# Half-lane products in a spectral token stage, a warm-up on a constant, and another order in the head of a fused LayerNorm, FFT-filter and GeGLU kernel

## Chip, cores and metric

The kernel runs on one core of a Trainium2 chip. The metric is device time in microseconds (us), the median of several executions. A core has TensorE (PE, matrix products, with its weight loads shown as PEld), VectorE (DVE), ScalarE (ACT), GpSimd (POOL) and SyncE (SP). The engines run on their own instruction streams, in order, and wait for each other with semaphores. In this kernel SP issues nearly all transfers; ACT issues a few at the start.

## The reference, cut to what matters

`A_x` is 2048 rows (tokens) of 512. It is normalised per row; the result `xn` goes two ways: through a 2-D real FFT, a product with a complex filter and the inverse FFT (A), and through a gated layer with 1792 hidden columns (B). The sum of `x`, A and B is stored.

```python
def _A_ref(x, w_r, w_i):
    X = rfft2(x.astype(f32), axes=(-2, -1))
    X = X * (w_r + 1j * w_i)
    return irfft2(X, s=(S, D), axes=(-2, -1)).astype(bf16)

def _B_ref(x, w_gate, w_up, w_down):
    g = einsum("bsd,df->bsf", x, w_gate)
    u = einsum("bsd,df->bsf", x, w_up)
    return einsum("bsf,fd->bsd", gelu_tanh(g) * u, w_down)

xn = layernorm(x)            # per row, eps 1e-5, no scale or shift
return x + _A_ref(xn, A_w_r, A_w_i) + _B_ref(xn, B_w_gate, B_w_up, B_w_down)
```

## The kernel before

**Planner.** The kernel function doesn't write the instruction streams directly. It lists operations with `op(engine, cost, fn, reads, writes, tiles, key, after, due)`. `_Sched.run` then plays through a model of the engines: of the operations that can start soonest on an engine (within `SLACK`), it takes the one with the least `due`, or, without one, the least readiness time plus `key`. Readiness of a PE operation of the spectral way gets `MARGIN` (1.0) on top once the model's time is past 12. A transfer (`dma`) goes through one modelled pipe of `RATE` bytes per us, and its end is the pipe's. `after` and the list `gate` add dependences: every SP load made after an entry in `gate` waits for that entry. The order found is emitted; at run time the engines follow it and wait on semaphores, whatever the model thought of times.

**Data.** The 2048 rows are 16 blocks of 128 rows (`x[:, s]`, partition = row within the block). Each block gets statistics (`stats`: L520, L521 on DVE), an inverse root (`root_act`: L525 on ACT and the reciprocal L527 on DVE, for blocks 0 and 1; `root_pool`: L532 and L533 on POOL for the others) and is normalised into `specB` (`norm`, L537; block 0 in two halves in `first_half`, L570). The blocks 0 to 3 are turned on PE with the identity matrix (L567 and L550) and copied out of PSUM to `xnT` (L572, L555); blocks 4 to 15 are turned by transfers (`turn_dma`, L576 on SP).

**The head.** PE starts with products on a tile of zeros into a bank nobody reads (L476, "warming"): eight in `warms` and two more inside the loop over blocks 0 and 1. DVE makes that tile of zeros. ACT issues the load of the identity and the first quarter of the transform constants (`small[:, 0:2]`), then the first 384 columns of the two gated weights `wg` and `wu`. SP issues the row blocks 0 and 1, waits for the third warming product (`gate`), and issues blocks 2 and 3, columns 384 to 768 of `wg` and `wu`, rows 4 to 7, and so on. `first` (L737) makes the first three feature columns' products for blocks 0 and 1, one block at a time; then come the products of `gated` (L718), 256 or 512 rows wide, with gelu (L723; L751 in `first`) and a copy (L724; L752) on ACT and the product of both on DVE (L725; L753). `down` (L766) multiplies by `wd`. These gated and down products are the filler of PE's stream: they have keys above 1000 and are taken whenever nothing of the spectral way is due.

**The spectral way.** `mirror` and `fold` combine groups of four row blocks on DVE. `mirror(b)` subtracts two mirrored parts and turns the difference, for b > 0 with a transfer on SP (L592), into `odd[b]`; `fold(b)` uses `odd[b]` in two of its operations. The channel transform is on PE (L631). A first part of the token transform is done on DVE (the long series of L466, the line of the helper `tt`, and L809), the rest on PE in eight classes `v`: `f_t`, two 512-column products for v > 0 (L851), and four for v = 0 (L854), which holds the two special classes 0 and 8: lanes 0 to 63 and 64 to 127 of its four stationary matrices are for either, with zeros in the other half. ACT copies each class out (L859). Then the filter product on DVE, the inverse token transform on PE (L931, L932), a DVE series, and the inverse channel transform (L991). The columns 0 and 256 need sums and differences of filter values, `edge`, made on POOL (L864) and used in six small DVE operations per half (L898).

**The filter loads.** After the transposes SP loads `wd`, the token constants `tf`, the filter in 22 transfers (`W`, spans of 14 to 460 KB), nine small ones for special rows, and the inverse constants `ti`. `gate` holds them behind an operation in `mirror(3)`: `hold[16] = sch.ops[-2]`, the subtraction that feeds the transfer of `odd[3]`.

Of the kernel before, what the change touches and what calls it, by code (L numbers as in the profile page):

```python
# [15 lines left out]
P = 128  # L16
# [3 lines left out]
WARM = 8  # L20
HKEY = 1.5
NORM = 14.0, 1.5
# [117 lines left out]
class _Op:  # L140
    __slots__ = ("eng", "fn", "cost", "key", "lag", "reads", "writes", "preds", "tiles", "first", "end", "pos", "dma", "seq",
                 "extra", "due")


class _Sched:
# [11 lines left out]
    def op(self, eng, cost, fn, reads=(), writes=(), tiles=(), key=0.0, after=(), dma=0, lag=0.0, due=None):  # L157
        o = _Op()
        o.eng, o.fn, o.cost, o.key, o.dma, o.lag, o.due = eng, fn, cost, key, dma, lag, due
# [41 lines left out]
    def run(self):  # L201
# [15 lines left out]
        while todo:  # L217
# [26 lines left out]
            if o.dma:  # L244
# [104 lines left out]
def bass_parallel_sum__spectral_gfnet__glu_gated_geglu__prompt_kernel(  # L349
# [24 lines left out]
    with ExitStack() as es:  # L374
# [30 lines left out]
        zero = sb("zero", [512])  # L405
# [54 lines left out]
        def dma(q, dst, src, nbytes, wr=None, rd=None, key=0.0, after=(), cost=0.41, lag=0.0):  # L460
            after = tuple(after) + tuple(gate if q == "sp" else ())
            return op(q, cost, lambda e: e.dma_start(dst() if callable(dst) else dst.ap, src() if callable(src) else src.ap),
                      reads=rd if rd is not None else (), writes=wr if wr is not None else (), dma=nbytes, key=key, after=after, lag=lag)
# [6 lines left out]
        op("dve", 0.2, lambda e: e.memset(zero.ap, 0.0), writes=(zero,), key=-90)  # L470


        wt = _T("dn")

        def warm(key):
            return op("pe", 0.427, lambda e: e.matmul(ps_dn[:, :], zero.ap[:, 0:P], zero.ap, start=True, stop=True), reads=(zero,), tiles=(wt,), key=key)  # L476

        warms = [warm(-50) for _ in range(WARM)]


# [7 lines left out]
        def rows(lo, hi):  # L488
            return load("sp", x[:, lo:hi], xb[:, lo:hi, :], (hi - lo) * 131072, key=next(k))
# [33 lines left out]
        def root_act(s0, n, key):  # L523
# [3 lines left out]
            op("dve", 0.09, lambda e: e.reciprocal(rs.ap[:, sl], rs.ap[:, sl]), reads=(rs[:, sl],), writes=(rs[:, sl],), key=key)  # L527
# [29 lines left out]
        def first_half(h):  # L557
# [14 lines left out]
            op("dve", 0.21, lambda e: e.tensor_copy(o.ap, bank()), writes=(o,), tiles=(t,), key=-70.0)  # L572
# [11 lines left out]
        odd = {}  # L584
# [22 lines left out]
        def fold(b):  # L607
# [9 lines left out]
            tt(f[:, :, 2], f[:, :, 3], odd[b], SUB, 512, kk)  # L617
            tt(f[:, :, 3], f[:, :, 3], odd[b], ADD, 512, kk)
# [46 lines left out]
        for s in range(4, 16):  # L665
# [3 lines left out]
            if s % 4 == 3:  # L669
                mirror(s // 4)  # L670
                hold[16] = sch.ops[-2]
# [6 lines left out]
        gate.append(hold[16])  # L678
# [364 lines left out]
```

## Time and profile before

| | us |
|---|---|
| median of 3 runs | 171.83 (171.66 to 171.91) |
| the profiled execution | 172.02 |
| its span in the profile | 170.0 |
| DVE, ACT, POOL busy | 146.1, 106.0, 11.5 |
| first warming product starts | 1.17 |
| first product of `first` starts | 6.11 |
| first product of `gated` starts | 9.44 |
| products of L854 (class 0) | 65.8 to 66.8 |
| last product ends | 167.7 |

Three lines of the costliest groups and two of the transfers:

```profile
L718 PE MATMUL ps_gu<-xnT,wg 128*128 128x512 bf16 (+1 forms) x236 | 56.7, 363 | 0.0
L718 PE MATMUL ps_gu<-xnT,wu 128*128 128x512 bf16 (+1 forms) x236 | 56.7, 363 | 0.0
...
L520 DVE BATCH_NORM_STATS2 bst<-x_sb 128x6 f32<-128x512 bf16 x16 | 10.9, 684 | 2.6 <-DMA x_sb<-in_A_x_dram 2.6
...
wg<-in_B_w_gate_dram SPq DMA_DIRECT2D x2, 512.0 KB, 8.7
wu<-in_B_w_up_dram SPq DMA_DIRECT2D x2, 512.0 KB, 9.2
```

A group line reads: line, engine, operation, output <- inputs, shapes, count | total busy us, mean ns of one | idle time of the engine just before them and what ended it. Matmuls are pipelined: a 512-column product is shown with 0.379, but the next one starts 0.216 later, so what counts for PE's stream is the distance of the starts. A transfer line reads: output <- input, queue, count, size, and the median time from issue to landing.

### The profile page before, as it was taken

What the parts mean: (1) busy time and instruction counts of PE and PEld (TensorE: products, weight loads), DVE (VectorE), ACT (ScalarE), POOL (GpSimd) and SP (SyncE); (2) the same over time, 40 slices, a digit from 0 to 9 for tenths busy, and PEclk for the clock granted to TensorE, in tenths of its full rate; (3) what the DMA queues carried; (4) which work ended last, traced back from release to release, by engine and by line L of the source; (5) the groups of instructions that cost most, each with busy time, mean ns of one, the idle gap of its engine ahead of it and who ended that gap; (6) DMA issues with size and microseconds to landing.
All of it is one profiled execution on the core that took longest, in us unless ns stands there. A gap on an engine that the chain in (4) does not pass through costs nothing.

```text
span 170.0 us, 2695 instructions
## 1 busy us (share of the span) xinstructions
PE 166.2 (98%) x998; PEld 85.9 (51%) x998; DVE 146.1 (86%) x295; ACT 106.0 (62%) x173; POOL 11.5 (7%) x23
## 2 busy tenths in 40 slices
PE   7999999999999999999999999999999999999994
PEld 2588544445556444444444465554445664444453
DVE  2879999796945999999999999999999969963931
ACT  3478776573977758588854696795637896561000
POOL 2022242500000000400000000000000000000000
DMA  5999989974975435000000000000000002300321
GB/s 145 344 346 348 277 176 327 189 211 83 121 128 125 85 53 198 0 6 0 0 0 0 0 4 0 0 0 0 4 0 2 0 4 99 128 19 0 123 68 62
DMA packets 22239, 15.62 MB, mean 92 GB/s; under 512 B 9165, under 2 KB 21714, under 8 KB 22226
## 3 DMA queue, kind: packets, MB, share of 16 engines
q1 hardware_dynamic: 21026, 14.60, 38.0%
q10 hardware_dynamic: 1200, 0.85, 1.6%
q8 instruction: 8, 0.13, 0.3%
q14 instruction: 5, 0.04, 0.1%
HBM read 11.38 MB, written 2.10 MB: 79 GB/s over the span
## 4 chain that ended last, share of the span: by engine, by line
PE 95%; DMA 3%; DVE 1%; issue 0%; DVEq 0%
PE ps_gu L718 55%; PE ps_dn L766 21%; PE ps_sp L766 7%; DMA x_sb<-in_A_x_dram 3%; PE ps_sp L631 2%; PE ps_sp L991 2%; PE ps_sp L851 2%; PE ps_sp L931 1%; PE ps_sp L932 1%; PE ps_dn L476 1%; PE ps_gu L737 1%; PE ps_sp L854 1%; DVE bst L520 0%; PE ps_dn L737 0%; PE ps_sp L550 0%; DVE xnT L555 0%
## 5 line engine op out<-in xcount | busy, mean ns | idle before, releaser
L718 PE MATMUL ps_gu<-xnT,wg 128*128 128x512 bf16 (+1 forms) x236 | 56.7, 363 | 0.0
L718 PE MATMUL ps_gu<-xnT,wu 128*128 128x512 bf16 (+1 forms) x236 | 56.7, 363 | 0.0
L723 ACT ACTIVATE gg<-ps_gu 128x512 bf16<-128x512 f32 (+1 forms) x59 | 33.7, 571 | 14.3 <-PE ps_gu L718 12.1
L724 ACT ACTIVATE uu<-ps_gu 128x512 bf16<-128x512 f32 (+1 forms) x59 | 33.9, 574 | 10.5 <-PE ps_gu L718 10.2
L766 PE MATMUL ps_dn<-wd,hT 128*128 128x512 bf16 x168 | 39.0, 379 | 0.0
L466 DVE TENSOR_TENSOR specB<-specB 128x512 bf16<-128x512 bf16 (+2 forms) x58 | 33.1, 609 | 3.8 <-DMA specB<-specB 2.3
L718 PEld LDWEIGHTS ps_gu<-xnT,wu 128*128 128x128 bf16 x236 | 22.8, 98 | 23.2
L718 PEld LDWEIGHTS ps_gu<-xnT,wg 128*128 128x128 bf16 x236 | 22.6, 98 | 22.3 <-ACT uu L752 0.2
L766 PEld LDWEIGHTS ps_dn<-wd,hT 128*128 128x128 bf16 x168 | 16.2, 98 | 18.6
L725 DVE TENSOR_TENSOR hT<-gg,uu 128x512 bf16<-128x512 bf16 (+1 forms) x59 | 22.6, 393 | 1.7 <-ACT uu L724 1.6
L774 ACT ACTIVATE db<-ps_dn 128x512 bf16<-128x512 f32 x12 | 7.2, 597 | 17.7 <-PE ps_dn L766 17.7
L520 DVE BATCH_NORM_STATS2 bst<-x_sb 128x6 f32<-128x512 bf16 x16 | 10.9, 684 | 2.6 <-DMA x_sb<-in_A_x_dram 2.6
L466 DVE TENSOR_TENSOR specC<-specB 128x1024 bf16<-128x1024 bf16 (+2 forms) x18 | 12.4, 712 | 0.2
L766 PE MATMUL ps_sp<-wd,hT 128*128 128x512 bf16 (+2 forms) x70 | 12.3, 336 | 0.0
L466 DVE TENSOR_TENSOR specB<-specA 128x2048 bf16<-128x2048 bf16 x8 | 9.4, 1217 | 1.4 <-ACT specA L636 1.4
L466 DVE TENSOR_TENSOR specB<-specB,filt 128x2048 bf16<-128x2048 bf16 x8 | 9.4, 1219 | 0.0
L766 PEld LDWEIGHTS ps_sp<-wd,hT 128*128 128x128 bf16 x70 | 6.3, 98 | 6.1 <-DVE x_sb L777 0.2
L775 DVE TENSOR_TENSOR x_sb<-db,x_sb 128x512 bf16<-128x512 bf16 x12 | 5.0, 418 | 4.8 <-ACT db L774 4.7
L859 ACT ACTIVATE specA<-ps_sp 128x1024 bf16<-128x1024 f32 x8 | 8.0, 1035 | 1.5 <-PE ps_sp L851 1.3
L996 ACT ACTIVATE specB<-ps_sp 128x1024 bf16<-128x1024 f32 x8 | 7.8, 1031 | 0.4 <-PE ps_sp L991 0.4
L937 ACT ACTIVATE specC<-ps_sp 128x1024 bf16<-128x1024 f32 x8 | 7.8, 1034 | 0.3 <-PE ps_sp L932 0.3
L636 ACT ACTIVATE specA<-ps_sp 128x1024 bf16<-128x1024 f32 x8 | 7.8, 1031 | 0.0
(71 smaller groups left out, 128.9 us busy)
## 6 DMA issues: line engine op xcount, KB each, us to landing
out_dram<-x_sb SPq DMA_DIRECT2D x15, 128.0 KB, 1.8
wd<-in_B_w_down_dram SPq DMA_DIRECT2D x1, 1792.0 KB, 8.7
x_sb<-in_A_x_dram SPq DMA_DIRECT2D x3, 512.0 KB, 8.5
wg<-in_B_w_gate_dram SPq DMA_DIRECT2D x2, 512.0 KB, 8.7
wu<-in_B_w_up_dram SPq DMA_DIRECT2D x2, 512.0 KB, 9.2
toki<-c_ti SPq DMA_DIRECT2D x1, 768.0 KB, 4.7
tokf<-c_tf SPq DMA_DIRECT2D x1, 576.0 KB, 4.4
x_sb<-in_A_x_dram SPq DMA_DIRECT2D x4, 128.0 KB, 3.6
```

The lines of the kernel that those rows point to most:

```text
L466: return op("dve", c_tt(n), lambda e: e.tensor_tensor(o.ap, a.ap, b.ap, f), reads=(a, b), writes=(o,), key=key, **kw)
L520: op("dve", 0.61, lambda e: e.bn_stats(bst[:, s].ap, xs(s).ap), reads=(xs(s),), writes=(bst[:, s],), key=key, due=due, after=after)
L636: op("act", c_act(1024), lambda e, yv=yv, t=t: e.activation(yv.ap, spair(t).rearrange("p (s r i) -> p s i r", s=4, r=4), ACT.Copy), writes ...
L718: ins = e.matmul(gub(t, n), w.ap[:, dc, fc * P:(fc + 1) * P], xnT.ap[:, b, sl, dc, :], start=(dc == 0), stop=(dc == 3))
L723: op("act", c_act(n), lambda e: e.activation(gg.ap[:, gs.slot, 0:n], gub(g, n), ACT.Gelu_apprx_tanh), tiles=(g, gs), key=0.0)
L724: op("act", c_act(n), lambda e: e.activation(uu.ap[:, us.slot, 0:n], gub(u, n), ACT.Copy), tiles=(u, us), key=0.0)
L725: op("dve", c_tt(n), lambda e: e.tensor_tensor(hT.ap[:, h.slot, lo:lo + n], gg.ap[:, gs.slot, 0:n], uu.ap[:, us.slot, 0:n], MUL), tiles=(g ...
L766: ins = e.matmul(bank(), hT.ap[:, hs[(b, fc)].slot, sl * P:(sl + 1) * P], wd.ap[:, fc, lo:lo + n], start=(fc == 0), stop=(fc == NFC - 1))
L774: op("act", c_act(n), lambda e: e.activation(db.ap[:, d.slot, 0:n], bank(), ACT.Copy), tiles=(t, d), key=0.0)
L859: op("act", c_act(1024), lambda e, xv=xv, t=t: e.activation(xv.ap, spair(t), ACT.Copy), writes=(xv,), tiles=(t,), key=-0.5)
L937: op("act", c_act(1024), lambda e, gv=gv, t=t: e.activation(gv.ap, spair(t).rearrange("p (k x i) -> p k x i", k=4, x=4), ACT.Copy), writes ...
L996: op("act", c_act(1024), lambda e, rv=rv, t=t: e.activation(rv.ap, spair(t), ACT.Copy), writes=(rv,), tiles=(t,), key=-0.5)
```

## The change

Six things are changed together.

1. **Class 0.** The four products of `f_t` for v = 0 use only the 64 lanes that aren't zero: for i = 0, 1 and r = 0, 1 lanes 64r to 64r + 63 of the stationary matrix and of `H`. The order is now r inside i. The planner counts two products for it instead of four.
2. **Warming** multiplies a constant 1.0, which the framework keeps in a small tile set by POOL before the kernel starts, broadcast to 512 columns. The zero tile and its memset go. There are ten products of 512 columns and one of 256, all in `warms`; the two in the loop go. The gate of SP's third and later loads is the fourth warming product instead of the third.
3. **Loads.** The identity goes from ACT's queue to SP's, behind blocks 0 and 1. Four loads get a fixed landing time for the planner (`land`): these don't move the modelled pipe on.
4. **Order of statistics and roots.** Block 1's reciprocal root and block 0's get other keys, and block 0's reciprocal waits for block 1's statistics. Blocks 2 and 3 take their statistics after block 1 is normalised, turned and copied, and their roots on POOL are taken one by one. Statistics of blocks 4 to 15 wait for the norm of block 3. The norms' due times start at 15 instead of 14.
5. **Copies.** The two halves of block 0 are copied out of PSUM by ACT instead of DVE, and the first use of gelu (L643, which makes ACT load its table) waits for them.
6. **The filter loads' gate** is now the operation in `fold(3)` that subtracts `odd[3]`, thus behind the landing of its transfer (`turned[3]`).

```diff
-WARM = 8
+WARM = 10 * (512,) + (256,)
-NORM = 14.0, 1.5
+NORM = 15.0, 1.5
...
-            if o.dma:
+            if o.land:
+                o.end = o.land
+            elif o.dma:
                 pipe = max(pipe, st + 1.9) + o.dma / RATE
                 o.end = pipe + 0.4 + o.lag
...
-        op("dve", 0.2, lambda e: e.memset(zero.ap, 0.0), writes=(zero,), key=-90)
+        ones = nc.const_aps.tensor(1.0, (P, 512), BF16)
...
-            return op("pe", 0.427, lambda e: e.matmul(ps_dn[:, :], zero.ap[:, 0:P], zero.ap, start=True, stop=True), reads=(zero,), tiles=(wt,), key=key)
+            return op("pe", 0.000834 * n, lambda e: e.matmul(ps_dn[:, 0:n], ones[:, 0:P], ones[:, 0:n], start=True, stop=True), tiles=(wt,), key=-50)
-        warms = [warm(-50) for _ in range(WARM)]
+        warms = [warm(n) for n in WARM]
...
-        load("act", small[:, 0:2].rs([2 * P]), c_small.ap()[:, 0:2 * P], 65536, key=-9)
         for w, v in ((wg, wgv), (wu, wuv)):
-            wload("act", w, v, 0, 384, key=0.5)
+            wload("act", w, v, 0, 384, key=0.5, land=5.5 if w is wg else 6.4)
         rows(0, 1)
         rows(1, 2)
-        gate.append(warms[2])
+        load("sp", small[:, 0:2].rs([2 * P]), c_small.ap()[:, 0:2 * P], 65536, key=next(k))
+        gate.append(warms[3])
         for i in (2, 3):
-            rows(i, i + 1)
+            rows(i, i + 1, 6.3 + 0.3 * i)
...
-            op("dve", 0.09, lambda e: e.reciprocal(rs.ap[:, sl], rs.ap[:, sl]), reads=(rs[:, sl],), writes=(rs[:, sl],), key=key)
+            op("dve", 0.09, lambda e: e.reciprocal(rs.ap[:, sl], rs.ap[:, sl]), reads=(rs[:, sl],), writes=(rs[:, sl],), key=key, after=after)
...
-            op("dve", 0.21, lambda e: e.tensor_copy(o.ap, bank()), writes=(o,), tiles=(t,), key=-70.0)
+            op("act", 0.3, lambda e: e.activation(o.ap, bank(), ACT.Copy), writes=(o,), tiles=(t,), key=-70.0)
...
             tt(f[:, :, 2], f[:, :, 3], odd[b], SUB, 512, kk)
+            turned[b] = sch.ops[-1]
...
         stats(0, -60.0)
-        stats(1, -55.0, None, (sch.ops[-1],))
-        root_act(0, 1, -60.0)
-        root_act(1, 1, -58.0)
-        op("act", 1.5, lambda e: e.activation(tmp.ap, eps.ap, ACT.Gelu_apprx_tanh), reads=(eps, rs[:, 0:2]), writes=(tmp,), key=-30.0)
+        stats(1, -66.0, None, (sch.ops[-1],))
+        root_act(0, 1, -75.0, (sch.ops[-2],))
+        root_act(1, 1, -64.0)
         for h in range(2):
             first_half(h)
-        for s in range(2):
-            if s:
-                norm(s, -60.0)
-                turn(s, 1, -60.0)
-            warm(-30)
-            if s == 0:
-                stats(2, -30.0, None, (sch.ops[-2],))
-        stats(3, -30.0, None, (sch.ops[-2],))
-        root_pool(2, 2, -50.0)
+        op("act", 1.5, lambda e: e.activation(tmp.ap, eps.ap, ACT.Gelu_apprx_tanh), reads=(eps, xnT[:, 0, 0], rs[:, 0:2]), writes=(tmp,), key=-30.0)
+        norm(1, -60.0)
+        turn(1, 1, -60.0)
         for s in (2, 3):
+            stats(s, -58.0, None, (sch.ops[-1],))
+        for s in (2, 3):
+            root_pool(s, 1, -50.0)
             norm(s, -50.0)
+            early = sch.ops[-1]
             turn(s, 1, -50.0)
...
         for s in range(4, 16):
-            stats(s, 0.0, STAT[0] + STAT[1] * (s - 4))
+            stats(s, 0.0, STAT[0] + STAT[1] * (s - 4), (early,))
...
-                hold[16] = sch.ops[-2]
...
-        gate.append(hold[16])
+        gate.append(turned[3])
...
-                for r in range(2):
-                    if v:
-                        ins = e.matmul(spb(t, r), tf.ap[:, 2 + 2 * v + r], H.ap[:, hh[r]], start=True, stop=True)
-                    else:
-                        for i in range(2):
-                            ins = e.matmul(spb(t, r), tf.ap[:, 2 * r + i], H.ap[:, hh[i]], start=(i == 0), stop=(i == 1))
+                for r in range(2) if v else ():
+                    ins = e.matmul(spb(t, r), tf.ap[:, 2 + 2 * v + r], H.ap[:, hh[r]], start=True, stop=True)
+                for i in range(0 if v else 2):
+                    for r in range(2):
+                        l = slice(64 * r, 64 * r + 64)
+                        ins = e.matmul(spb(t, r), tf.ap[l, 2 * r + i], H.ap[l, hh[i]], start=(i == 0), stop=(i == 1))
                 return ins
-            op("pe", (2 if v else 4) * mm(512), f_t, reads=(H[:, hh[0]], H[:, hh[1]], tf), tiles=(t,), lag=0.1)
+            op("pe", 2 * mm(512), f_t, reads=(H[:, hh[0]], H[:, hh[1]], tf), tiles=(t,), lag=0.1)
```

More of the change, by code (lines that the diff above doesn't have):

```diff
@@ L141 @@
     __slots__ = ("eng", "fn", "cost", "key", "lag", "reads", "writes", "preds", "tiles", "first", "end", "pos", "dma", "seq",
-                 "extra", "due")
+                 "extra", "due", "land")
 class _Sched:
@@ L155, in pool, with op @@
         self.pools[name] = n
-    def op(self, eng, cost, fn, reads=(), writes=(), tiles=(), key=0.0, after=(), dma=0, lag=0.0, due=None):
+    def op(self, eng, cost, fn, reads=(), writes=(), tiles=(), key=0.0, after=(), dma=0, lag=0.0, due=None, land=None):
         o = _Op()
-        o.eng, o.fn, o.cost, o.key, o.dma, o.lag, o.due = eng, fn, cost, key, dma, lag, due
+        o.eng, o.fn, o.cost, o.key, o.dma, o.lag, o.due, o.land = eng, fn, cost, key, dma, lag, due, land
         o.reads, o.writes, o.tiles = reads, writes, [(t, False) for t in tiles]
@@ L404, in bass_parallel_sum__spectral_gfnet__glu_gated_geglu__prompt_kernel @@
         t2 = sb("edge2", [2, 4, 2])
-        zero = sb("zero", [512])
         eps = sb("eps", [1], F32)
@@ L458, in bass_parallel_sum__spectral_gfnet__glu_gated_geglu__prompt_kernel, with dma @@
         gate = []
-        def dma(q, dst, src, nbytes, wr=None, rd=None, key=0.0, after=(), cost=0.41, lag=0.0):
+        def dma(q, dst, src, nbytes, wr=None, rd=None, key=0.0, after=(), cost=0.41, lag=0.0, land=None):
             after = tuple(after) + tuple(gate if q == "sp" else ())
             return op(q, cost, lambda e: e.dma_start(dst() if callable(dst) else dst.ap, src() if callable(src) else src.ap),
-                      reads=rd if rd is not None else (), writes=wr if wr is not None else (), dma=nbytes, key=key, after=after, lag=lag)
+                      reads=rd if rd is not None else (), writes=wr if wr is not None else (), dma=nbytes, key=key, after=after, lag=lag, land=land)
         def tt(o, a, b, f, n, key=0.0, **kw):
@@ L468, in bass_parallel_sum__spectral_gfnet__glu_gated_geglu__prompt_kernel, with warm @@
         ADD, SUB, MUL = ALU.add, ALU.subtract, ALU.mult
-        op("dve", 0.2, lambda e: e.memset(zero.ap, 0.0), writes=(zero,), key=-90)
+        ones = nc.const_aps.tensor(1.0, (P, 512), BF16)
         wt = _T("dn")
-        def warm(key):
-            return op("pe", 0.427, lambda e: e.matmul(ps_dn[:, :], zero.ap[:, 0:P], zero.ap, start=True, stop=True), reads=(zero,), tiles=(wt,), key=key)
-        warms = [warm(-50) for _ in range(WARM)]
+        def warm(n):
+            return op("pe", 0.000834 * n, lambda e: e.matmul(ps_dn[:, 0:n], ones[:, 0:P], ones[:, 0:n], start=True, stop=True), tiles=(wt,), key=-50)
+        warms = [warm(n) for n in WARM]
         def load(q, dst, src, nbytes, **kw):
@@ L487, in bass_parallel_sum__spectral_gfnet__glu_gated_geglu__prompt_kernel, with rows @@
         k = iter(np.arange(0.0, 1.0, 0.001))
-        def rows(lo, hi):
-            return load("sp", x[:, lo:hi], xb[:, lo:hi, :], (hi - lo) * 131072, key=next(k))
-        load("act", small[:, 0:2].rs([2 * P]), c_small.ap()[:, 0:2 * P], 65536, key=-9)
+        def rows(lo, hi, land=None):
+            return load("sp", x[:, lo:hi], xb[:, lo:hi, :], (hi - lo) * 131072, key=next(k), land=land)
         for w, v in ((wg, wgv), (wu, wuv)):
-            wload("act", w, v, 0, 384, key=0.5)
+            wload("act", w, v, 0, 384, key=0.5, land=5.5 if w is wg else 6.4)
         rows(0, 1)
         rows(1, 2)
-        gate.append(warms[2])
+        load("sp", small[:, 0:2].rs([2 * P]), c_small.ap()[:, 0:2 * P], 65536, key=next(k))
+        gate.append(warms[3])
         for i in (2, 3):
-            rows(i, i + 1)
+            rows(i, i + 1, 6.3 + 0.3 * i)
         for w, v in ((wg, wgv), (wu, wuv)):
@@ L521, in stats, with root_act @@
             op("dve", 0.11, lambda e: e.bn_aggr(bag[:, s].ap, bst[:, s].ap), reads=(bst[:, s],), writes=(bag[:, s],), key=key, due=due)
-        def root_act(s0, n, key):
+        def root_act(s0, n, key, after=()):
             sl = slice(s0, s0 + n)
@@ L582, in bass_parallel_sum__spectral_gfnet__glu_gated_geglu__prompt_kernel @@
         z = R3(0, [16, 4, P])
-        odd = {}
+        odd, turned = {}, {}
         def mirror(b):
```

## The prediction

> **What bounds the kernel now.** I read the page first, then the chain of waits in order of time, then the timeline of the first 10 us, then the rows around the token stage and the filter loads.
>
> ```profile
> PE 166.2 (98%) x998; PEld 85.9 (51%) x998; DVE 146.1 (86%) x295; ACT 106.0 (62%) x173; POOL 11.5 (7%) x23
> ...
> PE 95%; DMA 3%; DVE 1%; issue 0%; DVEq 0%
> ```
>
> PE is busy 98% of the span and carries 95% of the chain that ends last. So a change counts if it removes PE work or a gap in PE's stream, and hurts if it makes a new gap. The chain (start, length, what) shows where gaps are:
>
> ```profile
> 2.67 4.26 DMA x_sb<-in_A_x_dram
> ...
> 7.01 0.69 DVE bst L520
> 7.71 0.33 DVE xnT L555
> ...
> 8.09 1.07 PE ps_gu L737 x16
> ...
> 12.18 26.83 PE ps_gu L718 x152
> ...
> 65.91 0.86 PE ps_sp L854 x4
> ...
> 155.57 12.14 PE ps_sp L766 x70
> ```
>
> At 8.09 PE waited for the copy of the second row block, which stood behind the statistics of the third (L520), which waited for its load: a gap of 0.26 (the last product before it starts at 7.78 and takes a slot of 0.056). From 8.09 the chain hardly leaves PE until 167.7. Between 9.4 and 12 the matmul starts show three more small gaps, 0.05 + 0.07 + 0.02; from 12 on the starts follow each other without one. So time = when the steady stream begins + PE's work + new gaps.
>
> **The token stage.** Class 0 makes four products of 512 columns at L854: 4 x 0.216 (0.86 / 4 from the chain). Half of each stationary matrix is zero, so the change multiplies 64 lanes each, lanes 0-63 and 64-127 in turn.
>
> ```profile
> L854 PE MATMUL ps_sp<-specC,tokf x4: 379/379/379, 65.8 to 66.4; 128*128 128x512 bf16 x4
> ```
>
> If both halves of a pair overlap, four slots become two: -0.43. No row of before shows a 64-lane product, so I bound it. Above: no overlap, 0. A product lasts 0.379 and the next starts after 0.216, so 0.163 is its tail; if the array had to empty when the shape changes, going in and coming back cost 2 x 0.163 = 0.33, which leaves -0.10 with overlap and +0.33 without. The bounds are -0.43 and +0.33. The two banks of a pair and the two halves of the lanes are disjoint, which speaks for overlap; I take -0.25, about the middle of the two overlapping cases.
>
> The Trainium skill, TensorE: Matmul & The Clock Gate, section "Part 3: Packing small matmuls", says that products in different row groups start about 4 ns apart; by it alone this term is -0.42. The Trainium skill, TensorEngine Tiling (Array Packing), section "Key Properties", says that a change of the tiling mode drains the engine, which speaks against this change; by it the term would be about -0.10. No row of before shows either.
>
> **The head, up to the first products.** Warming: POOL's constants are set by 0.42 and PE is let go at 0.70, so it no longer waits for DVE's memset (1.17): about 0.45 earlier. Ten and a half products at the 0.427 spacing of L476 take 4.48 and end near 5.2, before the first transposes (5.44 now), so this is costed at nothing. The spacing falls from 0.427 to the full rate at about 5.0, 3.85 after the warming began. If this came a stretch later than the first real products, the 24 products of the first row block would go at twice their 0.056: +1.3 at most; with an earlier start I leave it at 0. The SP gate moves from the third warming product to the fourth, but these start 0.43 earlier: the loads of rows 2 and 3 are issued at 2.67 as now. The identity load moves from ACT's queue to SP's, behind rows 0 and 1: issued about 1.6, it fits before that gate, and landing 2.4 later as now, or 3.0 as row 1 does, it is there by 4.6, before the transposes. ACT's sqrt table load (2.29 to 3.58) moves up by 0.4 and stays hidden until 4.24.
>
> Three things make the first products (6.11 now) later. (a) The reciprocal L527 must now wait for the second bn_stats to finish (4.94); now it is issued at 4.85 while that ends: +0.10 for the chain L527, L570. (b) The two copies out of PSUM go to ACT, where 256 columns take 0.38 (L751), against 0.29 on DVE (L572): +0.09. (c) The first row load now shares the DMA with a 384 KB weight load instead of the 64 KB of constants; that load has 768-byte packets, and one for one with the row's 1 KB packets this is up to +0.15; I take 0.1. Together +0.3: first product at about 6.4.
>
> In exchange DVE is free for the norm of row block 1, so its four transposes (L550, 0.22) fill the wait between the halves (0.14 now), and its copy L555 runs before L520 of block 2: at about 7.3 instead of 8.03. First block, transposes and second block are 48 x 0.056 + 0.22 = 2.9 without a gap: from 6.4 they end at 9.3, against 9.44 now: -0.14. The three later gaps (0.14) go if ACT and the loads keep up. Statistics of blocks 2 and 3 start 0.3 later (7.3 for 7.01), but the roots on POOL are taken one by one (L533 took 0.71 for two, from 9.37 to 10.08), so the transposes of block 2 come near 9.7 and those of block 3 near 10.6, where all eight come at 10.77 now; their blocks are read from about 12.4 on, so nothing is late. The gelu table load (1.28, L643) moves behind the ACT copies, to about 6.7 to 8.2; the first gelu is at 8.74 now, so it stays hidden by 0.4.
>
> What is late next is the second weight load of `wu`:
>
> ```profile
> 9.44 0.60 PE L718 MATMUL ps_gu<-xnT,wg 128*128 128x256 bf16 x4
> 9.92 0.60 PE L718 MATMUL ps_gu<-xnT,wu 128*128 128x256 bf16 x4
> ```
>
> It is issued at 3.99 and lands 5.8 later, 9.79; the row at 9.92 is the one that waits for it. PE would ask for it at 9.74. By the view of windows the DMA moved 186, 307 and 208 GB/s in the half-microseconds from 2.0 to 3.5, and about 345 after; the earlier issue of the weights (0.72 for 1.11) fills some of that, up to (159 + 38 + 137) GB/s x 0.5 us / 345 = 0.48 us. I take the landing 0.1 earlier. Sum for the head: -0.2; bounds +0.15 (the load stays and row 0 is late) and -0.35 (all gaps gone, no (c)).
>
> **The later gate of the filter loads.** SP's loads of the filter now wait for the subtraction that uses the last mirrored transpose (L592), not for the operation that feeds it.
>
> ```profile
> 40.55 1.22 SPq L462 DMA_DIRECT2D filt<-in_A_w_r_dram  x2
> 41.81 1.25 SPq L592 DMA_TRANSPOSE specB<-specB  x1
> ...
> 47.11 0.41 DVE L725 TENSOR_TENSOR hT<-gg,uu 128x512 bf16<-128x512 bf16 x1
> 49.78 0.88 DVE L466 TENSOR_TENSOR specB<-specB 128x512 bf16<-128x512 bf16 x2 [2.25 <-DMA specB<-specB]
> ```
>
> The transpose took 7.9 us to land behind filter loads; the least of its kind is 2.5. Issued at 40.55 it lands at 43.1 and DVE's 2.25 of waiting goes. That alone is worth nothing at the end, since PE had other work there. But the loads start only after the subtraction: 47.5 if DVE's order stays, 45.5 if the planner uses the 1.78 of idle before 42.70 for these folds. All 32 loads of the filter and the inverse constants queue behind that on SP, 5.0 to 7.0 later than at 40.55. Who waits for them:
>
> ```profile
> 68.29 2.12 POOL L864 TENSOR_TENSOR edge<-filt 128x16 bf16<-128x16 bf16 x2 [35.41 <-DMA filt<-in_A_w_r_dram]
> ...
> 76.14 0.26 DVE L898 TENSOR_TENSOR edge<-specA,edge 128x16 bf16<-128x16 bf16 x2
> ...
> 97.09 0.24 DVE L898 TENSOR_TENSOR specA<-edge 128x4 bf16<-128x4 bf16 x2
> ...
> 98.13 0.22 PE L931 MATMUL ps_sp<-toki,specA 128*128 128x128 bf16 x1
> ```
>
> POOL's edges end at 70.41 and are used at 76.14: 5.7 of cover. Behind L898 stands everything on DVE up to 97.33, without idle; PE takes it 0.8 later. With a shift of 5.0 to 5.7 it costs nothing: that is my value. With 7.0 it is the rival below. Four loads with a landing time given (1.0 MB) no longer fill the planner's own DMA pipe, which therefore expects later loads up to 3.1 earlier (at its 340 KB per us). Where it then puts work ahead of its data, an engine waits: for rows 4-7 (landing at 11.29, used at 12.37) the cover is 1.1; the one place without cover is the `wu` load above. The norms' due times (15 for 14) and the statistics held until the norm of block 3 only reorder DVE behind that: 0.
>
> **Sum.** -0.25 - 0.2 = -0.45. The profiled execution took 172.02 (span 170.0, 2.0 around it), 0.19 above the median of the runs, 171.83; I take the difference off the median: **171.4**.
>
> **Rivals.**
> *Late filter (slower).* Place: L864, then L898 on DVE. If the loads start at 47.5, edges end at 77.4, DVE is 1.2 late from L898 on, the inverse products L931 can start at 97.33 + 1.2 = 98.53 instead of 98.13: +0.4 against before whatever was won earlier, 172.2. It decides once the shift passes 5.7 + 0.8 = 6.5 (start after 47.1), and from 6.1 on it eats the gain. If L898 also stands earlier in DVE's order, more is lost. For it: DVE has no idle between 76 and 97. Against: the fold can move ahead, and the transpose no longer sits among the loads.
> *One gain only (no change).* If the array empties at both changes of shape, the two tails of 0.163 leave -0.10 at L854, and with the head -0.3: 171.5. (That it drains is the rule of the Trainium skill, TensorEngine Tiling (Array Packing), "Key Properties".) Or `wu` lands at 9.79 and the head gives 0.05: -0.25 - 0.05 = -0.3, 171.5. For it: the wait at 9.92 exists now.
> *The pair doesn't do what it says.* No overlap: token stage 0, head alone -0.2: 171.6, in the same class.
>
> **Chances.** A difference under 0.2% (0.34 us) can't be told from none. Forecast 0.50 (faster by over 0.2%), one gain or none 0.20 (same), late filter 0.30 (slower). The likeliest case has its own range, 171.05 (head -0.35, token -0.43) to 171.5; to hold 8 in 10 the range reaches into the late filter: 171.05 to 172.3.
>
> **What would show it.** Right: L854's four products with starts that span about 0.43 (two of them nearly together); no PE gap near 8; L555 before the second L520 pair; first PE row before 0.8; the filter's first SP issue before 46.5 and no DVE wait at L898. Wrong: a DVE wait for POOL's edges at L898 with a PE gap at L931; a gap of 0.16 before or after L854; a PE wait for `wu` near 9.8; products at half rate after 5.5.

## The result, and the profile after

The changed kernel takes 173.78 us (median of 6 runs, 173.14 to 175.12), the kernel before 171.87 beside it (6 runs, 171.66 to 172.21). The ratio is 1.0119, with a 95% interval of 1.0082 to 1.0156: slower by 1.2%, some 1.9 us, where 171.4 and a gain were forecast. The profiled execution took 173.69 with a span of 171.9; the span before was 170.0. Lines have moved by three: L715 is now the line of `gated`, L734 of `first`, L851 of class 0.

From the page after: busy time of each engine, the clock granted to TensorE in 40 slices, and the shares of the chain that ended last.

```profile
PE 165.6 (96%) x986; PEld 87.2 (51%) x999; DVE 146.0 (85%) x292; ACT 106.6 (62%) x175; POOL 10.4 (6%) x25
...
PEclk9889999999999999999999999999999999999999
...
PE 94%; DMA 3%; issue 1%; SPq 0%; ACT 0%; DVE 0%
```

PE's work is nearly unchanged (986 products are recorded for 999 weight loads, so 13 records are missing), but it fills 96% of a longer span. The second and third slices, 4.3 to 12.9 us, are below full clock; before, all forty were 9. So the loss is in the head. The chain of waits after, from its first load on (start, length, what):

```profile
1.63 4.93 DMA smallc<-c_small
6.57 0.14 issue
6.70 0.28 PE ps_sp L567 x2
```

`smallc` is the tile with the identity. Its load now stands at the head of the chain: issued at 1.63 on SP, it lands 4.93 later. Before, a row load stood there. PE's timeline after (start, length to the last end, line, tiles, shapes, count, and in brackets the idle time and what ended it):

```profile
0.76 3.76 PE L476 MATMUL ps_dn<-const-bfloat16-1.0 128*128 128x512 bf16 x11 [0.76 <-PEq L1025]
6.70 0.49 PE L567 MATMUL ps_sp<-smallc,specB 128*128 128x128 bf16 x4 [2.18 <-DMA smallc<-c_small]
7.54 0.58 PE L550 MATMUL ps_sp<-smallc,specB 128*128 128x128 bf16 x4 [0.34 <-ACT xnT L572]
7.92 1.06 PE L734 MATMUL ps_gu<-xnT,wg 128*128 128x128 bf16 x8
...
11.74 0.60 PE L715 MATMUL ps_gu<-xnT,wg 128*128 128x256 bf16 x4
```

The same engine before:

```profile
5.44 0.54 PE L567 MATMUL ps_sp<-smallc,specB 128*128 128x128 bf16 x4
...
7.16 0.61 PE L737 MATMUL ps_gu<-xnT,wu 128*128 128x128 bf16 x8
```

After, PE is idle from 4.52 to 6.70. Then eight products take 1.06 (at 7.92), where before eight without a wait among them took 0.61 (at 7.16): 0.107 from start to start instead of 0.056. From 10.3 on, they are at full rate again. The chain names only the wait that ended last. A second one ended just before it, on DVE (timeline before, then after):

```profile
4.85 0.15 DVE L527 RECIPROCAL rstd<-rstd 128x1 f32<-128x1 f32 x1
```

```profile
5.23 0.69 DVE L520 BATCH_NORM_STATS2 bst<-x_sb 128x6 f32<-128x512 bf16 x1 [0.90 <-DMA x_sb<-in_A_x_dram]
5.96 0.16 DVE L527 RECIPROCAL rstd<-rstd 128x1 f32<-128x1 f32 x1
```

The rows of block 1 land at 5.13 instead of 4.13. Block 0's reciprocal now stands behind block 1's statistics, so it comes at 5.96 instead of 4.85, and the first half of block 0 is normalised at 6.51 instead of 5.38, 0.06 before the identity lands.

The view of windows after gives the clock (from:to, length, busy time of PE, PEld, DVE, ACT, POOL with counts, the granted clock, DMA share, GB/s):

```profile
4.00:5.00 1.00, 0.52 (x3) 0.10 (x1) 0.29 (x2) 0.29 (x1) 0.00 (x0) 1.00 1.09 357
5.00:7.00 2.00, 0.30 (x4) 0.24 (x4) 1.70 (x7) 0.29 (x1) 0.00 (x0) 0.97 1.11 340
7.00:10.00 3.00, 2.66 (x26) 2.49 (x25) 2.02 (x5) 2.15 (x4) 0.29 (x2) 0.50 1.10 335
10.00:12.00 2.00, 2.00 (x34) 1.98 (x32) 0.98 (x4) 0.92 (x3) 1.32 (x3) 0.93 1.10 348
```

0.50 all through 7 to 10, and 0.97 and 0.93 in the neighbours: half clock from 6.88 (0.12 of two us at one half) to 10.28. Before, each such window shows 1.00.

The sum of it. The first `gated` product starts at 11.74 instead of 9.44: +2.30. Class 0 gives back 0.23, and the small gaps between 9.4 and 12 (0.14) are gone: +1.93, against +1.9 in the span.

Class 0 does what it says (timeline of PE, before, then after):

```profile
65.75 1.03 PE L854 MATMUL ps_sp<-specC,tokf 128*128 128x512 bf16 x4
66.61 1.03 PE L718 MATMUL ps_gu<-xnT,wg 128*128 128x512 bf16 x4
```

```profile
66.26 0.60 PE L851 MATMUL ps_sp<-specC,tokf 64*128 64x512 bf16 x4
66.80 1.04 PE L715 MATMUL ps_gu<-xnT,wg 128*128 128x512 bf16 x4
```

The four products and the step to the next line took 0.86 before and 0.54 after, with 0.096 more ahead of them.

### The profile page after: what moved, and what is told of

Read it like the earlier page. It is cut to its first block, busy times and chain, and to the rows that moved or that the text cites. A ratio compares the mean times of both kernels' runs of the same rounds, so it can differ in the third digit from the quotient of the medians.

```text
span 171.9 us, 2682 instructions
## 1 busy us (share of the span) xinstructions
PE 165.6 (96%) x986; PEld 87.2 (51%) x999; DVE 146.0 (85%) x292; ACT 106.6 (62%) x175; POOL 10.4 (6%) x25
## 4 chain that ended last, share of the span: by engine, by line
PE 94%; DMA 3%; issue 1%; SPq 0%; ACT 0%; DVE 0%
PE ps_gu L715 55%; PE ps_dn L763 21%; PE ps_sp L763 7%; DMA smallc<-c_small 3%; PE ps_sp L988 2%; PE ps_sp L632 2%; PE ps_sp L847 2%; PE ps_gu L734 2%; PE ps_sp L928 1%; PE ps_sp L929 1%; PE ps_dn L734 1%; PE ps_sp L550 1%; SPq L463 0%; PE ps_sp L851 0%; ACT xnT L572 0%
## 5 line engine op out<-in xcount | busy, mean ns | idle before, releaser
L715 PE MATMUL ps_gu<-xnT,wg 128*128 128x512 bf16 (+1 forms) x236 | 56.7, 363 | 0.0
L715 PE MATMUL ps_gu<-xnT,wu 128*128 128x512 bf16 (+1 forms) x236 | 56.7, 363 | 0.0
L763 PE MATMUL ps_dn<-wd,hT 128*128 128x512 bf16 x156 | 36.6, 379 | 0.6
L715 PEld LDWEIGHTS ps_gu<-xnT,wu 128*128 128x128 bf16 x236 | 22.9, 98 | 23.1
L715 PEld LDWEIGHTS ps_gu<-xnT,wg 128*128 128x128 bf16 x236 | 22.6, 98 | 22.1 <-ACT uu L721 0.4
L722 DVE TENSOR_TENSOR hT<-gg,uu 128x512 bf16<-128x512 bf16 (+1 forms) x59 | 23.2, 399 | 2.2 <-ACT uu L721 2.2
```

What stands on the lines that cost most here:

```text
L715: ins = e.matmul(gub(t, n), w.ap[:, dc, fc * P:(fc + 1) * P], xnT.ap[:, b, sl, dc, :], start=(dc == 0), stop=(dc == 3))
L722: op("dve", c_tt(n), lambda e: e.tensor_tensor(hT.ap[:, h.slot, lo:lo + n], gg.ap[:, gs.slot, 0:n], uu.ap[:, us.slot, 0:n], MUL), tiles=(g ...
L763: ins = e.matmul(bank(), hT.ap[:, hs[(b, fc)].slot, sl * P:(sl + 1) * P], wd.ap[:, fc, lo:lo + n], start=(fc == 0), stop=(fc == NFC - 1))
```

## The experiments

Twelve more kernels were built. *Theory 1*: the identity's load and block 1's rows are late because they queue behind the weight loads, and *1a*: PE's idle time then costs it the clock. Its rivals lay the time to the other edits of the head: roots and statistics, copies, the pairs, the filter gate. Ratios are to the kernel before, run beside it on the same chip, with 95% intervals.

| kernel | us (range) | ratio | first L567 | first `gated` |
|---|---|---|---|---|
| changed kernel | 173.78 (173.14–175.12) | 1.0119 [1.0082, 1.0156] | 6.70 | 11.74 |
| e1, identity first on ACT | 171.78 (171.67–171.96) | 0.9986 [0.9975, 0.9996] | 5.64 | 9.50 |
| e2, before + pairs | 171.85 (171.37–172.09) | 0.9983 [0.9971, 0.9996] | 5.48 | |
| e8, same, other order | 171.79 (171.41–171.99) | 0.9982 [0.9972, 0.9993] | | |
| e3, long warming | 172.63 (172.31–173.37) | 1.0041 [1.0026, 1.0057] | 6.61 | 10.35 |
| e4, root first | 175.25 (174.52–176.29) | 1.0191 [1.0157, 1.0225] | 6.73 | 13.32 |
| e7, identity first on SP | 175.49 (175.39–176.59) | 1.0213 [1.0186, 1.0241] | 7.81 | 13.04 |
| e7b, e7 and e4 | 175.54 (175.20–176.51) | 1.0211 [1.0183, 1.0238] | 6.81 | 12.41 |
| e13, both weights later | 172.26 (171.94–174.43) | 1.0035 [1.0004, 1.0066] | 5.61 | 10.25 |
| e14, `wu` later | 173.63 (172.09–173.79) | 1.0095 [1.0077, 1.0113] | 6.41 | 10.16 |
| e12, e1 and copies on DVE | 172.29 (171.96–172.67) | 1.0012 [1.0001, 1.0023] | 5.60 | 9.39 |
| e10, e1 and e4 | 172.61 (172.44–173.20) | 1.0028 [1.0015, 1.0040] | 5.19 | 9.71 |
| e9, before + filter gate | 172.18 (171.95–172.69) | 1.0002 [0.9993, 1.0011] | 5.57 | |

**The identity back on ACT's queue.** It stands ahead of both weight loads there; the rest of the change stays.

```diff
-        load("sp", small[:, 0:2].rs([2 * P]), c_small.ap()[:, 0:2 * P], 65536, key=next(k))
+        load("act", small[:, 0:2].rs([2 * P]), c_small.ap()[:, 0:2 * P], 65536, key=-9)
```

> The changed kernel with the identity load put back where it was, first on ACT's queue, so that the weight loads on ACT go out 0.4 later again; all else as changed. Theory 1 (the loads' order): the identity lands near 3.1 and row block 1 near 4.1 as in before, the first transposes run near 5.6, PE isn't idle for 2 us and keeps its full rate, and the first product of gated starts near 9.3: 171.3 to 171.6, a ratio of about 0.998. Theory 2 (the added wait of the reciprocal and the copies on ACT): the first transposes stay later than 6 and the time above 172.8.

PE's timeline of this kernel:

```profile
5.64 0.54 PE L567 MATMUL ps_sp<-smallc,specB 128*128 128x128 bf16 x4 [0.24 <-DVE specB L570]
6.60 0.38 PE L550 MATMUL ps_sp<-smallc,specB 128*128 128x128 bf16 x4 [0.42 <-ACT xnT L572]
6.82 0.61 PE L734 MATMUL ps_gu<-xnT,wg 128*128 128x128 bf16 x8
...
9.50 0.60 PE L715 MATMUL ps_gu<-xnT,wg 128*128 128x256 bf16 x4
```

One load on another queue takes the ratio from 1.0119 to 0.9986. The identity lands at 3.12, PE waits for it no more, the products are at full rate, and the kernel is a little faster than the one before. Theory 1 holds. Block 1's rows come earlier too, at 3.70 instead of 5.13, since the weights now go out 0.4 later; so this run can't tell which of the two late loads held the head. The time stayed 0.2 above the 171.58 that the forecast's sum would give (172.03 beside it, less 0.45).

**The pairs alone, on the kernel before**, and once more with both products of one half behind each other (the two loops of the new lines exchanged):

```diff
-                for r in range(2):
-                    if v:
-                        ins = e.matmul(spb(t, r), tf.ap[:, 2 + 2 * v + r], H.ap[:, hh[r]], start=True, stop=True)
-                    else:
-                        for i in range(2):
-                            ins = e.matmul(spb(t, r), tf.ap[:, 2 * r + i], H.ap[:, hh[i]], start=(i == 0), stop=(i == 1))
+                for i in range(0 if v else 2):
+                    for r in range(2):
+                        l = slice(64 * r, 64 * r + 64)
+                        ins = e.matmul(spb(t, r), tf.ap[l, 2 * r + i], H.ap[l, hh[i]], start=(i == 0), stop=(i == 1))
```

> The kernel before with the half-lane products of class 0 alone. The four products of class 0 take 0.86 of PE's stream before. Overlap with a short loss at the change of shape (what the changed kernel's trace suggests): their stretch and the gap ahead of it take about 0.64, so about -0.2 to -0.3 us: 171.6. No overlap: 171.9 or more. The planner counts two products and may set the filler in another order; if a wait comes of that, it shows as a PE gap and the time is above 171.9 although the class itself is shorter.

> The kernel before with the half-lane products of class 0, but the two of one half one after the other instead of the halves in turn; every engine's order is that of the run with the pairs alone. If the gain comes from two halves running at once: the four products now start 0.216 apart except where the half changes, the class takes about 0.65 to 0.86 plus 0.19 for the two changes of shape, and the time is 0.2 to 0.4 above the run with the pairs in turn (172.0 to 172.2). If a half-lane product is simply cheaper: the same as in turn.

Both gain 0.17% to 0.18%, 0.3 us. In the first the four start at 65.891, 65.894, 66.117 and 66.120: two at once, 3 ns apart. The last full product ahead of them takes 0.312 of PE's stream instead of 0.216, and the last of the four 0.308: each change of shape costs 0.09 to 0.10. The block takes 0.63 for 0.86. In the second kernel the starts are 66.113, 66.120, 66.339 and 66.345, just as close, though 0.2 to 0.4 more time was expected there if two halves run at once. So the order in the program doesn't matter; whether PE took the other half ahead of its turn can't be read from the trace. The gain of e1 and of the pairs alone are the same within their intervals: with the identity on ACT, everything else in the change together is worth about nothing.

**Eight more warming products**, so that PE isn't idle while the identity is late; loads and order stay:

```diff
-        warms = [warm(n) for n in WARM]
+        warms = [warm(n) for n in WARM] + [warm(512, 0.0) for _ in range(8)]
```

> The changed kernel with eight more warming products behind the others (their output is read by nobody), the order of all else the same: they fill PE's idle time from 4.5 to about 6.3 and change no wait. Theory 1a (the late loads cost twice, first as idle time and then because PE's rate halves after it): the rate stays full, the 24 products of row block 0 take 1.34 instead of 2.6, and the time falls by about 1.2 to 172.6, with less scatter between runs. Theory 1b (only the lateness counts): no change, 173.8.

PE's timeline and the window of 7 to 10 us:

```profile
6.61 0.40 PE L567 MATMUL ps_sp<-smallc,specB 128*128 128x128 bf16 x4
...
10.35 0.60 PE L715 MATMUL ps_gu<-xnT,wg 128*128 128x256 bf16 x4
```

```profile
7.00:10.00 3.00, 2.56 (x47) 2.58 (x47) 2.18 (x6) 2.41 (x5) 0.59 (x2) 1.00 1.10 335
```

The transposes are as late as before (6.61), but the clock is 1.00 and from there to the first `gated` product it takes 3.74 instead of 5.04. So of the 2.30 in the head, 1.26 is the late first transposes (5.44 to 6.70), 1.30 the clock that the idle time cost, and 0.26 is won by the new order (4.00 before, 3.74 here). The ratio falls from 1.0119 to 1.0041, and the span by 1.4.

**Block 0's root ahead of block 1's statistics**, the edit that the prediction charged with 0.10:

```diff
-        stats(1, -66.0, None, (sch.ops[-1],))
-        root_act(0, 1, -75.0, (sch.ops[-2],))
+        root_act(0, 1, -75.0)
+        stats(1, -66.0, None, (sch.ops[-1],))
```

> The changed kernel with block 0's root and reciprocal ahead of block 1's statistics on DVE, so that block 0 no longer waits for the rows of block 1 (landed at 5.13); the planner sets a part of the later order anew. Theory 1 with two gates (rows of block 1 and identity, landed at 6.57): the normalised block 0 is ready near 5.3, but its transposes still wait for the identity until 6.6, so nothing much is won: 173.3 to 173.9. Theory 2 (the reciprocal's place is the cause): transposes near 5.4, time 171.6 to 172.

```profile
6.73 0.59 PE L567 MATMUL ps_sp<-smallc,specB 128*128 128x128 bf16 x4 [1.33 <-DMA smallc<-c_small]
7.58 1.09 PE L734 MATMUL ps_gu<-xnT,wg 128*128 128x128 bf16 x8 [0.26 <-ACT xnT L572]
...
9.75 0.63 PE L550 MATMUL ps_sp<-smallc,specB 128*128 128x128 bf16 x4
```

The normalised block was ready at 5.10, and PE still waited for the identity until 6.73: that wait is the identity's alone, and it is enough to hold the transposes. The time was missed by over 1 us. Warming never came to full rate here (starts 0.427 apart to its end), and the products went 0.107 apart until 13.2. Why the clock came so late is open.

**The identity first on SP**, alone and with the roots of the last experiment:

```diff
+        load("sp", small[:, 0:2].rs([2 * P]), c_small.ap()[:, 0:2 * P], 65536, key=next(k))
         rows(0, 1)
         rows(1, 2)
-        load("sp", small[:, 0:2].rs([2 * P]), c_small.ap()[:, 0:2 * P], 65536, key=next(k))
```

> The changed kernel with the identity load first on SP's queue, ahead of row blocks 0 and 1; the weights still go out first on ACT's. Tells the identity from the rows. If the late identity alone is the cause: transposes right after the normalised block 0, and most of the 1.9 us comes back (172.2 or less). If the rows of block 1 hold block 0 too, through the second statistics and the reciprocal that wait for them: these rows still land near 5.1 or later, the normalised block 0 is ready no earlier than 6.2 to 6.5, the transposes start near 6.5 instead of 6.7, PE still idles for about 2 us, and the time stays within 0.5 of 173.8.

> The same, and block 0's root and reciprocal ahead of block 1's statistics, so that block 0 waits for neither. If these two waits are the whole cause of the late first transposes, they now run near 5.1 to 5.4, before or as early as in the kernel before (5.44), PE's idle time is under 0.7 and the rate stays full; block 1 is then the late one (its rows land near 5.1 to 5.5, its transposes run near 7.3), so 171.7 to 172.4. If the time stays above 173, something else holds the head.

```profile
7.81 0.54 PE L567 MATMUL ps_sp<-smallc,specB 128*128 128x128 bf16 x4 [2.56 <-DVE specB L570]
...
9.04 1.06 PE L734 MATMUL ps_gu<-xnT,wg 128*128 128x128 bf16 x8
```

Both are slower still, which was not expected. The identity is early, but in e7 PE waits until 7.81 for the normalised block 0 (L570), which stands behind block 1's statistics. The identity lands at 2.91, but now block 0's rows, issued at 1.12, land at 4.80, and block 1's, issued at 1.61, at 6.38. Whichever load is second on SP lands at 4.8 to 5.2 and whichever is third at 6.4 to 6.6, rows or constants: near `wg` (4.42) and `wu` (6.04), which ACT issued 0.4 ahead of each. So what counts is a load's place among the loads of both queues.

**The weights later.** If so, holding ACT's weights back must bring all SP loads back, with no engine's order changed. In e14 only `wu` gets the new dependence:

```diff
         for w, v in ((wg, wgv), (wu, wuv)):
-            wload("act", w, v, 0, 384, key=0.5, land=5.5 if w is wg else 6.4)
+            wload("act", w, v, 0, 384, key=0.5, after=(warms[2],), land=5.5 if w is wg else 6.4)
```

> The changed kernel, with ACT's two 384 KB weight loads held until the third warming product (about 2.0 us) instead of 0.72; every engine's order stays the same, the identity stays third on SP. Theory 1 (a load queues behind the 384 KB loads issued before it on another queue): identity and block 1's rows no longer have the weights ahead of them; issued at 1.6 and 1.2 they land by 3.3 and 3.9, the first transposes start by 5.6 instead of 6.70, PE's idle time shrinks and the clock stays full; the weights then land at about 5.6 and 7.2 and the first products may wait for them: 171.9 to 172.7. Rival (SP's third load is slow in itself, as the constants' 512-byte packets or the queue are): the identity still lands at 5.5 or later and the time stays at 173 or above.

> The changed kernel with only the second of ACT's two weight loads (wu, 384 KB) held until the third warming product, so that it is issued at about 2.2, behind the identity (1.63) but long before the identity's turn comes; wg stays at 0.72, every engine's order stays. Both theories agree with all runs so far. Order of issue: whatever was issued first is served first over all queues; the identity is ahead of wu, lands at about 5.4, the first transposes start by 5.7 and the time is 171.9 to 173.0. Turns: the two queues are served in turn, one whole load each (row block 0, wg, row block 1, wu, identity); wu still goes ahead of the identity, which lands at 6.2 or later with the first transposes at 6.4 or later, and the time stays at 173.2 or above.

Three views of transfers, the changed kernel, then e13, then e14 (tile and source, queue, count, size, us from issue to landing):

```profile
wu<-in_B_w_up_dram ACTq DMA_DIRECT2D x1, 384.0 KB, 5.4
...
smallc<-c_small SPq DMA_DIRECT2D x1, 64.0 KB, 4.9
```

```profile
smallc<-c_small SPq DMA_DIRECT2D x1, 64.0 KB, 2.0
```

```profile
wu<-in_B_w_up_dram ACTq DMA_DIRECT2D x1, 384.0 KB, 5.8
...
smallc<-c_small SPq DMA_DIRECT2D x1, 64.0 KB, 3.5
```

With both weights behind it, the same load, third on the same queue, lands in 2.0 instead of 4.9; with only `wg` ahead, in 3.5 (at 5.17, and `wu`, issued 0.6 behind it, at 8.00). That is order of issue over both queues, not turns of one load each, as far as `wu`, issued at 2.23, was queued when the identity's turn came some time before 5.17. Strict order of issue isn't the whole rule either: in e14 the rows of block 2, which SP issued 0.42 behind `wu`, landed at 7.17, 0.8 ahead of it.

e14 also shows the second wait by itself. Its identity is there at 5.17, but the first transposes, expected by 5.7, start at 6.41:

```profile
6.41 0.54 PE L567 MATMUL ps_sp<-smallc,specB 128*128 128x128 bf16 x4 [1.17 <-DVE specB L570]
```

PE waits for the normalised block 0, which stands behind block 1's statistics, and block 1's rows land at 4.97, behind `wg`. So either late load alone puts the transposes at 6.4 (rows, e14) or 6.7 (identity, e4). Only with both early do they start near 5.6 (e1, e13). e13's transposes start at 5.61 and its price is what was expected, a wait for the late `wu`:

```profile
8.23 0.62 PE L734 MATMUL ps_gu<-xnT,wu 128*128 128x128 bf16 x8 [0.52 <-DMA wu<-in_B_w_up_dram]
```

The identity of e14 fits the first theory, but the median, 173.63, is past the 173.0 expected of it. The profiled execution took 172.09 with the clock at 1.00, the four others 173.49 to 173.79; in e13 seven runs took 171.94 to 172.42 and three 173.71 to 174.43. The step of 1.5 is about the 1.30 that the half clock costs. The mean granted clock of every execution is on record: in e13 it is 0.99 in the three long ones and 1.00 in the seven others, and 3.41 us at half clock make 0.99 of some 172. So e13 loses the clock in some executions and not in others. In e14 two of the four long ones read 0.99 and two 1.00, so there it is shown for two alone.

**The copies back on DVE, and block 0's root first, each on top of e1.** Without the identity's wait these two terms can be seen.

```diff
-            op("act", 0.3, lambda e: e.activation(o.ap, bank(), ACT.Copy), writes=(o,), tiles=(t,), key=-70.0)
+            op("dve", 0.21, lambda e: e.tensor_copy(o.ap, bank()), writes=(o,), tiles=(t,), key=-70.0)
```

> The kernel with the identity back on ACT's queue, and the two copies of block 0 out of PSUM back on DVE (all else as changed). With the copies on ACT the first products started at 6.82 in that run, 0.9 after the last transposes of block 0; a copy there takes 0.38 and hands over more slowly than the 0.29 on DVE. If that is a cost on PE's path: first products near 6.3 and the first of gated about 0.2 earlier (9.3 for 9.50), then partly given back at the second load of wu (9.68): 171.5 to 171.7 against 171.78. If the DVE's free time was worth it: the norm of block 1 is later and the time is 171.9 or more.

> The changed kernel with the identity back on ACT's queue (as in the first experiment) and block 0's reciprocal no longer behind block 1's statistics. Theory (a) of the prediction (that wait costs 0.10 of the first products): the first transposes come 0.1 to 0.2 earlier than the 5.64 of the first experiment and the time is 171.6 to 171.75. Rival (block 1 is what bounds the head there, its square root then standing behind the copies on ACT): block 1's transposes come later than 6.60 and the time is 171.8 to 172.2.

PE's timeline of the kernel with the root first (e10), and of the one with the copies on DVE (e12):

```profile
5.19 0.63 PE L567 MATMUL ps_sp<-smallc,specB 128*128 128x128 bf16 x4
6.08 0.86 PE L734 MATMUL ps_gu<-xnT,wg 128*128 128x128 bf16 x8 [0.26 <-ACT xnT L572]
...
8.36 0.40 PE L734 MATMUL ps_gu<-xnT,wg 128*128 128x128 bf16 x4 [0.30 <-DVE xnT L555]
...
13.78 0.61 PE L715 MATMUL ps_gu<-xnT,wg 128*128 128x256 bf16 x4 [0.49 <-DVE xnT L555]
```

```profile
6.27 0.77 PE L734 MATMUL ps_gu<-xnT,wg 128*128 128x128 bf16 x8
...
13.48 0.61 PE L715 MATMUL ps_gu<-xnT,wg 128*128 128x256 bf16 x4 [0.31 <-DVE xnT L555]
```

Both bring block 0 earlier than e1 (first product at 6.08 and 6.27 instead of 6.82), and both end later, by some 0.7 and 0.4 by their ratios (1.0028 and 1.0012 for 0.9986). With the root first, block 1's statistics come later, its transposes at 7.45 instead of 6.60, and PE waits before the second block; that was the rival. In both PE waits near 13 for the copy of a later block (L555); in e1 it doesn't wait there. So the wait for block 1's statistics and the copies on ACT, taken as costs in the prediction, earn more than they cost, at least in the order that the planner then makes of the rest: the waits near 13 are a part of that order.

**The later filter gate alone**, on the kernel before: `gate.append(turned[3])` for `gate.append(hold[16])`.

> The kernel before with the later gate of the filter loads alone. The sum's term 0 (5.7 us of cover at POOL's edges): the 2.25 us wait of DVE near 49.8 goes, the small DVE operations with the edges wait under 0.5 us, no PE gap near 98, and the time is within 0.1% of before. Rival, late filter: a wait of 1 us or more at the edges, a PE gap near 98 and 172.2 or more.

The timelines of SP, POOL and DVE:

```profile
47.88 10.93 SPq L462 DMA_DIRECT2D filt<-in_A_w_r_dram  x11
```

```profile
74.69 1.80 POOL L865 TENSOR_TENSOR edge<-filt 128x16 bf16<-128x16 bf16 x2 [41.80 <-DMA filt<-in_A_w_r_dram]
```

```profile
76.41 0.30 DVE L899 TENSOR_TENSOR edge<-specA,edge 128x16 bf16<-128x16 bf16 x2 [0.19 <-POOL edge L865]
```

The loads start 7.3 later, the edges end 6.1 later (76.49 for 70.41), and DVE waits 0.19 for them, which reaches nobody: 1.0002. On DVE the cover of 5.7 is passed by these 0.19; PE's products at L932 still start at 98.12, as before (98.13). The changed kernel has the same 0.19 there.

## Why the prediction was wrong, and where it was right

**The step that failed** is the landing of SP's second and third load in the head. For the identity the prediction says: "landing 2.4 later as now, or 3.0 as row 1 does, it is there by 4.6, before the transposes". It took the time from issue to landing as the load's own, from rows in which nothing large was issued well ahead of it. In the change ACT issues its 384 KB loads 0.4 earlier, ahead of SP's second and third load. The identity, issued behind both, took 4.93 and landed at 6.57. Block 1's rows landed at 5.13 instead of 4.13, and through them term (a), the reciprocal's wait for the second statistics, came to 1.11 instead of 0.10 (5.96 for 4.85). Either of the two alone holds the first transposes, by 1.0 (e14, 6.41 for 5.44) or 1.3 (e4, 6.73). The prediction saw that row 0 would share the DMA with a weight load (+0.1; it was 3.39 for 3.27, right) and didn't carry this on to the two loads behind it, where it mattered.

**The clock.** "If this came a stretch later than the first real products ... +1.3 at most; with an earlier start I leave it at 0." The size was right (1.30), the case was not thought of: full rate did come, earlier than forecast (the warming ends at 4.52, not 5.2), and was then lost, since PE was idle for 2.18 us. Costing the warming at nothing named no cover for the case that the next work is late. Nor is 3.85 from the first warming product to full rate a fixed time: with the same warming from 0.76, the trace's clock record has full rate from 3.40 in e13, 3.47 in the changed kernel, 4.49 in e3, 5.91 in e1 and 6.56 in e10, and by its starts e4 has it only near 13.2.

**Term by term.** Token stage: forecast -0.25, measured -0.23; as the forecast was about the middle of two bounds, so close a hit is luck. The two changes of shape cost 0.19 together, less than the two tails of 0.33 that the low case assumed, and the pairs do start together, as the Trainium skill has it in TensorE: Matmul & The Clock Gate, "Part 3: Packing small matmuls" (about 4 ns; here 3). Head without the late identity (e1): forecast -0.2; measured -0.08 (first `gated` product +0.06, the gaps of 0.14 gone), within its bounds. Term (a), forecast 0.10, was too small even with early rows: in e10, without that wait, the first transposes come 0.45 earlier than in e1 (5.19 against 5.64), though taking it away loses. Term (b), the copies on ACT: 0.38 each as said. `wu`'s second load: 9.75 for 9.79 where 0.1 was forecast. The filter gate: 0, right, but for another reason than given. The prediction let the late filter decide from a shift of 6.5 on; alone, the loads shift by 7.3 and the edges by only 6.1, which is why nothing is lost. The loads start at 50.05 in the changed kernel and 47.88 alone, past the 46.5 that was to show it right, and there was to be no wait at the edges where 0.19 are seen. The late-filter rival, with 77.4 for the end of the edges from a start at 47.5, was too high by 0.9. No rival named a late load in the head; the one slower case with a price stood on the filter, so the slower end of the range, 172.3, was built from the wrong place.

**What stays open:** why the clock came so late in e4, whether the clock also explains the two long executions of e14 that read 1.00, and by what rule the DMA chooses between the two queues.

## What to carry to other kernels

A small load that all first work waits for goes ahead of every large load, on whichever queue: in these runs it mostly landed with or behind the large loads that another queue had issued 0.4 ahead. Before moving a load, list the loads of all queues in order of issue, and price each by what lies ahead of it. Follow every late load to the first work that needs it: here two loads were late, and bringing back one alone would have won little. And when warming products end before the first real work is there, the idle time can be paid twice, once as a wait and once in clock: let the warming reach past the latest arrival.

## What was not expected of the hardware

**Loads of two queues are served mostly in order of issue.** A load of 64 or 128 KB that SP issued 0.4 behind a 384 KB load of ACT landed together with that load or behind it (6.57 and 6.59; 5.13 and 4.76; in e7 4.80 and 4.42, 6.38 and 6.04), and in e14 well ahead of a load issued 0.6 behind it. Where it was issued only 0.06 behind (block 1's rows in e1), it landed first, at 3.70 against 5.14. Other exceptions are block 2's rows: issued 0.43 behind `wg` in e13, 0.42 behind `wu` in e14 and 1.0 behind `wu` in e8 and e12, they landed 0.2 to 0.8 ahead of it. The Trainium skill, DMA: Bandwidth & Descriptors, "Queues, rings and completion order", says that each DMA engine goes round between its queues packet by packet. Turns of small pieces don't agree with the changed kernel: by 4.3 its DMA had moved some 640 KB (149 GB/s on average from the start), which is the 320 KB of SP's first three loads with as much from ACT beside them, yet the identity landed at 6.57. How much one turn takes here, no trace shows.

**Two us of idle time can lose the clock for 3.4.** Warming starts come 0.427 apart up to 3.27 and 0.22 apart from 3.59; the half clock lasts from 6.88 to 10.28. The stretches from change to change are 3.4 us each (the trace's clock record has the first at 3.47), and PE was idle for 2.2 of the one before the clock fell. In such stretches PE was busy for 1.23 here, 0.82 in e7 and 1.58 in e7b, and the clock fell; in e13 and e14 it was busy for 1.98 and 1.93, and the clock stayed. So the line lay between 1.58 and 1.93 in these five executions, and since the stretches lie elsewhere in each execution, the same idle time can cost the clock once and not the next time. The Trainium skill, TensorE: Matmul & The Clock Gate, "Part 1: The HAM clock gate", names a free-running window of 3413 ns, which agrees; its idle window for going back to half rate would not be this one, since PE worked for a third of it.

**The granted clock of the windows isn't the whole story.** It shows 1.00 while warming products start 0.427 apart, and 1.00 from 8 to 12 us of e4, where 128-column products start 0.107 apart. The record has no entry at all in e4, and none before 3.47 in the changed kernel. The distance of the starts is the safer reading.
